# The row shares of an attention pair are turned as 128 rows and spread by four DMAs, and the plan gives out the attention's PSUM banks

## The chip, the cores and the metric

The kernel runs on one core of a Trainium2 chip. The metric is the device time of one execution in microseconds (us); the profile tells the span from the first to the last instruction, which is a little shorter. The engines are TensorE (PE; its weight loads stand as PEld), VectorE (DVE), ScalarE (ACT), GpSimd (POOL) and SyncE (SP), which here only issues DMAs.

## The reference

Causal attention over 2 batches, 12 heads, 448 tokens and head size 64, then two gated layers on the 896 tokens of 768 features. All data are float32.

```python
scores = q @ k.T / 8, masked above the diagonal
attn = exp(scores - max); attn = attn / (sum(attn) + 1e-9)
x = (attn @ v) with the heads side by side             # 896 x 768
x = (silu(x @ w_gate) * (x @ w_val)) @ w_out           # 768 -> 1536 -> 768
h = x @ w_in;  out = (h * clip(h + 3, 0, 6) / 6) @ w_out2   # 768 -> 2048 -> 768
```

## The kernel before

The kernel keeps float32 accuracy by cutting each operand into a rounded part and a rest (`hi`, `lo`) and summing three products. It has two stages: `attention()` and `mlps()`. The change is in the first.

Attention works on 12 pairs: two heads of one batch. A pair p goes through steps in a software pipeline over t:

- *Turn* (t = p - 2): q and k of the pair come in by DMA (`nat`), DVE turns them in 32 x 32 blocks (`f`), POOL or ACT rounds them (`qh`, `kh`) and POOL takes the rests (`ql`, `kl`). For the first two pairs PE does the turning.
- *Scores* (`sc`, t = p): 24 matmuls into PSUM banks, in three groups of rows. DVE adds the mask and takes the row maxima (`e<-sc,mask`), ACT takes the exponentials (`e<-e,m`) and the row sums (`s`).
- *Turned exponentials* (`tp`, t = p + 1): 20 PE transposes of 112 x 112, copied out of PSUM by ACT or DVE (`et`).
- *Product with v* (`pv`, t = p + 2): 16 matmuls into one bank. It is not yet divided by the row sums.
- *Shares* (`shares`, in `pv_parts`, between the second and the third product): POOL adds the epsilon to the 112 x 8 sums (`r`), DVE takes the reciprocal, POOL spreads each of the 8 columns over 64 columns (`rb`, 112 x 512), PE turns that in four transposes (`tr<-keep,rb`), and ACT copies the bank to SBUF (`rs`, 128 x 448). So rs holds, for each of the 128 rows (two heads of 64 features), the shares of the 448 tokens.
- *Last*: DVE multiplies the pv bank by rs (`xa<-pv,rs`, `xb<-pv,rs`) and frees the bank; rounding and rest give `x`, the first layer's operand.

From t = 7 on, four weight units of the first layer are also made ready (`first_unit`: one DMA `raw`, ACT, two shifts and joins on DVE, rounding, rest), and 36 of that layer's matmuls (`mm`) are woven into the last steps, as `ahead_parts`.

The order of the work is made before the kernel runs. `Plan.op` writes down each operation with its cost on the engines that may do it, what it reads and writes; `Plan.run` is a list scheduler that places them in time, on each engine the one that is due first, with a price for a change of kind on PE (`NEXT`, `WEIGHT`) and idle PE time in the first 21 us filled with matmuls of zeros. Every engine then runs its own list strictly in that order, so an instruction that waits holds up what stands behind it. SP's list of DMAs is also in that order. Before, an operation's PSUM bank is fixed when it is written down, from the list `idle` in program order.

Of the kernel before, what the change touches and what calls it, by code (L numbers as in the profile page):

```python
# [21 lines left out]
EB = 4  # L22
# [28 lines left out]
SLIP, WEIGHT = 0.1, 60.0  # L51
# [3 lines left out]
SOON = 6.0  # L55
CASTS = ("pool", "act")
HOLD, HEAD, LEND = 0.1, 3.0, 0.0
# [6 lines left out]
SHARED = ("vec", "pool")  # L64

# [16 lines left out]
class Spot:  # L82

    def __init__(self, make=None, place=None, real=None, ready=0.0):
        self.make, self.place, self.real, self.ready, self.after = make, place, real, ready, set()

# [6 lines left out]
class Plan:  # L93

    def __init__(self, in_order=("pe", "sp"), start=START, hold=0.0, ahead=0.0, alone=None, lend=None):
        self.ops, self.uses, self.on_place = [], {}, {}
        self.soon, self.kinds, self.by, self.alone = [], [], [], alone
# [3 lines left out]
    def op(self, where, call, reads=(), writes=(), port=False, wire=0.0, soon=None, kind=None, by=None):  # L101

        i, before, ready = len(self.ops), set(), 0.0
        for writing, spots in ((False, reads), (True, writes)):
            for s in spots:
                spot, part = s if isinstance(s, tuple) else (s, None)
                if spot not in self.uses:
                    self.uses[spot] = []
                    old = self.on_place.get(spot.place)
                    if old is not None:  # L110
                        spot.after = {j for _, j, _ in self.uses[old]}
                    if spot.place is not None:
                        self.on_place[spot.place] = spot
                before |= spot.after
                ready = max(ready, spot.ready)
                one = spot.place is not None and spot.place[0] is self.alone
# [5 lines left out]
        self.ops.append((where, call, before, ready, port, wire + LANDING if wire else 0.0))  # L122
        self.soon.append(soon)
        self.kinds.append(kind)
        self.by.append(by)

    def run(self, emit):
# [3 lines left out]
        for i, (_, _, before, _, _, _) in enumerate(ops):  # L131
            for j in before:
                after[j].append(i)
# [3 lines left out]
        for i, (where, _, _, _, _, _) in enumerate(ops):  # L137
            if "pe" in where:
                due[i] = clock
                clock += where["pe"]  # L140
        for i in reversed(range(n)):
# [6 lines left out]
            if self.by[i] is not None:  # L148
                due[i] = min(due[i], clock - self.by[i])
        left = [len(ops[i][2]) for i in range(n)]  # L150
        at = [
            ops[i][3] if self.soon[i] is None else max(ops[i][3], due[i] - self.soon[i]) for i in range(n)
        ]
        free_at, port_free, wire_free = dict(self.start), 0.0, 0.0
# [3 lines left out]
        while waiting:  # L158
            best = None
            for e in free_at:  # L160
# [14 lines left out]
                starts = {i: max(free_at[e], at[i], port_free if shared and ops[i][4] else 0.0) for i in mine}  # L175
                t = min(starts.values())
# [18 lines left out]
            if e == "pe":  # L195
                last = self.kinds[i]
                if self.fill is not None and t < self.fill[2]:
                    for x in range(int((t - free_at[e]) / self.fill[0] - 0.5)):
                        placed.append((free_at[e] + x * self.fill[0], len(placed), n, e))
                        filled += 1  # L200
# [5 lines left out]
            placed.append((t, len(placed), i, e))  # L206
            lag = LAG[e]
            if ops[i][5]:
                wire_free = max(wire_free, t + cost) + ops[i][5] - LANDING
                lag = wire_free + LANDING - t - cost  # L210
# [6 lines left out]
        for t, _, i, e in sorted(placed):  # L217
            emit(t, e, ops[i][1] if i < n else self.fill[1])
        self.placed = sorted(placed)
# [3 lines left out]
def tile_attention_glu_mlp(  # L223
# [118 lines left out]
    def attention():  # L342
        with ExitStack() as st:
# [4 lines left out]
            nc.vector.memset(zeros, 0.0)  # L348
            make_identity(nc, ident)
# [11 lines left out]
            plan = Plan(in_order=(), start=AT_START, hold=HOLD, ahead=HEAD, alone=banks, lend=LEND)  # L361
# [9 lines left out]
            def bank(use):  # L371
                n = idle.pop(0)
                return Spot(lambda: banks.tile([128, 512], F32, tag=f"bank{n}", name=use), (banks, n)), n
# [3 lines left out]
            def zero(e):  # L377
                e.matmul(idler()[:, :128], zeros, zeros, start=True, stop=True)

            plan.fill = ZERO, zero, UNTIL  # L380
# [11 lines left out]
            natq, natk, set_of, v_of, e_of, et_of, s_of = {}, {}, {}, {}, {}, {}, {}  # L392
            PAIR = 2 * S * D

            def load(p, src):
# [3 lines left out]
                for row, rows, head, half_ in ((32, 64, 0, 0), (0, 32, 0, 1), (96, 32, 1, 1)):  # L399
# [9 lines left out]
                        writes=[(t, row)], wire=0.6 if rows == 64 else 0.53, soon=SOON,  # L409
# [54 lines left out]
            def split(p, src, f):  # L464
# [4 lines left out]
                    lambda e: move(e, hi(), f()), reads=[f], writes=[hi], port=True,  # L469
# [4 lines left out]
                    reads=[f, hi], writes=[lo], port=True,  # L474
# [134 lines left out]
            def tp_parts(p):  # L609
# [29 lines left out]
                return [lambda j=j, ks=ks: turns(j, ks) for ks in ((0,), (1,), (2, 3)) for j in range(2)]  # L639

            def pv_parts(p):
# [4 lines left out]
                vt, ets, sm = v_of[p], et_of.pop(p), s_of.pop(p)  # L646
# [16 lines left out]
                def shares():  # L663
                    r, rb = take("r", 2, [C, 2, NC]), take("rb", 1, [C, NC, 2, D])
                    tr, bn = bank("tr")
                    rs = box["rs"] = take("rs", 1, [128, S])
                    op(
                        {"pool": 0.22},
                        lambda e: e.tensor_scalar(out=r(), in0=sm(), scalar1=EPS, scalar2=None, op0=ALU.add),
                        reads=[sm], writes=[r],  # L670
                    )
                    op({"vec": 0.19}, lambda e: e.reciprocal(out=r(), in_=r()), writes=[r])
                    op(
                        {"pool": 0.72},
                        lambda e: e.tensor_copy(
                            rb(), r().rearrange("p j c -> p c j").unsqueeze(3).to_broadcast([C, NC, 2, D])
                        ),
                        reads=[r], writes=[rb], port=True,
                    )

                    def work(eng):
                        for c in range(NC):
                            eng.transpose(
                                tr()[:, c * C : (c + 1) * C], rb()[:, c].rearrange("p j d -> p (j d)"), ident[:C, :C]
                            )

                    op({"pe": 0.4}, work, reads=[rb], writes=[tr], kind="tp")
                    op({"act": 0.44}, lambda e: e.copy(rs(), tr()[:, :S]), reads=[tr], writes=[rs])
                    idle.append(bn)

                def last():
                    o, rs = box["o"], box["rs"]
# [19 lines left out]
                        reads=[(t, b), (x, 0)], writes=[(x, 1)], by=BY_END if p == NPAIR - 1 else None, port=True,  # L712
# [8 lines left out]
                return [lambda kc=kc: product(kc) for kc in range(2)] + [shares] + [  # L721
# [5 lines left out]
            def first_unit(src, a, b, ready, by):  # L727
# [8 lines left out]
                op(  # L736
                    {"sp": 1.0},
                    lambda e: e.dma_start(out=raw().rearrange("p a b two -> p a (b two)"), in_=src),
                    writes=[raw], wire=4.0,
                )  # L740
# [5 lines left out]
                    reads=[raw], writes=[w],  # L746
                )
                for g in range(2):
                    h = slice(g * a // 2, (g + 1) * a // 2)
                    op(  # L750
                        {"vec": 0.3},
                        lambda e, h=h: e.tensor_scalar(
                            out=w()[:, h].bitcast(U32), in0=w()[:, h].bitcast(U32), scalar1=3, scalar2=None,
                            op0=ALU.logical_shift_left,
                        ),
                        writes=[(w, g)], port=True,
                    )
                    op(
                        {"vec": 0.55},
                        lambda e, h=h: e.scalar_tensor_tensor(  # L760
                            out=w()[:, h].bitcast(U32), in0=raw()[:, h, :, 0], scalar=29, in1=w()[:, h].bitcast(U32),
                            op0=ALU.logical_shift_right, op1=ALU.bitwise_or,
                        ),
                        reads=[raw], writes=[(w, g)], port=True,
# [21 lines left out]
            def ahead_parts():  # L786

                def step(u, kk):
                    wh, wl = made[u]
                    if kk == 0:  # L790
                        early.append(bank("mm"))
                    t, _ = early[u]
# [51 lines left out]
            plan.run(lambda t, engine, call: call(by[engine]))  # L844

    def mlps():
# [5 lines left out]
        nc.vector.memset(half, 0.5)  # L852
        nc.vector.memset(floor, -0.484375)
# [185 lines left out]
        def plain(f, ws):  # L1039

            g1[f] = take([128, NT], F32, f"g{f}")
            for b in range(B):
                got = []
                if f == 0 and b == 0:
                    got = [(here((t(), (banks, f"bank{n}"))), n) for t, n in early]
# [609 lines left out]
```

## Time and profile before

| | us |
|---|---|
| median of 3 runs (541.24 to 541.77) | 541.48 |
| the profiled execution | 541.52 |
| its span | 539.7 |

The profiled execution lies within the spread of the runs, and 1.8 us of it lie outside the span. In the profile an engine's busy time counts instructions from start to end; PE's ends are modelled, so its time is better read from the starts of its phases and from the chain. "x20" counts instructions merged in one row, "a<-b" is the tile written and the tiles read, and "<-" behind an idle time names what ended it.

### The profile page before, as it was taken

The page shows a single profiled execution, that of the slowest core. Times are in us where ns is not written, and L with a number is a line of the kernel's source. Part 1 is how long each engine was busy: PE and PEld are TensorE (multiplying, and loading weights), DVE is VectorE, ACT ScalarE, POOL GpSimd, SP SyncE. Part 2 cuts the span into 40 slices and gives each one's busy share as a digit, 9 for nine tenths or more (in the row PEclk, how much of TensorE's full clock was granted, in tenths as well). Part 3 has the DMA queues.
Part 4 walks back from the last instruction along what each step waited for, and adds up shares of the span by engine and source line. Part 5 has one row for each costly group of instructions (what it writes and reads, how often), then busy time and mean ns, then how long its engine had stood idle before and what let it go on. Part 6 is the DMA issues. An engine that isn't in the chain of part 4 may idle for free.

```text
span 539.7 us, 9039 instructions
## 1 busy us (share of the span) xinstructions
PE 534.0 (99%) x3146; PEld 490.4 (91%) x3146; DVE 457.6 (85%) x932; ACT 417.6 (77%) x876; POOL 146.1 (27%) x163
## 2 busy tenths in 40 slices
PE   8999999999999999999999999999999999999997
PEld 6777778999999999999999999999999999999997
DVE  4999998999788778779998889989888957599982
ACT  5999996887787778589967788899898756696560
POOL 1799987304000000030030243222231300000311
PEclk9999999999999999999999999999999999999999
DMA  9998504355545433332002354365353155510112
GB/s 220 254 226 222 132 25 142 106 166 191 182 133 188 140 133 123 115 118 78 2 0 80 123 177 128 119 191 161 118 162 131 41 181 188 176 60 1 60 44 103
DMA packets 58990, 69.34 MB, mean 128 GB/s; under 512 B 16960, under 2 KB 52544, under 8 KB 58944
## 3 DMA queue, kind: packets, MB, share of 16 engines
q1 hardware_dynamic: 58016, 68.53, 42.7%
q8 instruction: 25, 0.41, 0.3%
q10 hardware_dynamic: 928, 0.23, 0.2%
q14 instruction: 21, 0.17, 0.1%
HBM read 65.99 MB, written 2.75 MB: 127 GB/s over the span
## 4 chain that ended last, share of the span: by engine, by line
PE 97%; DVE 1%; DMA 1%; issue 0%; SPq 0%; DVEq 0%
PE mm L76 83%; PE pv L76 5%; PE tp L76 4%; PE sc L76 4%; PE tr L76 1%; DMA nat<-in_k_dram 1%; DVE out L76 0%; DVE e L76 0%; SPq L76 0%; DVE ql L76 0%; DVE kl L76 0%; PE zero L76 0%; DVE m L76 0%; DVEq L76 0%
## 5 line engine op out<-in xcount | busy, mean ns | idle before, releaser
L76 PE MATMUL mm<-x,a 128*128 128x448 f32 x396 | 85.9, 363 | 0.0
L76 PE MATMUL mm<-x,s 128*128 128x448 f32 x378 | 80.6, 363 | 0.0
L76 PEld LDWEIGHTS mm<-x,a 128*128 128x128 f32 x396 | 74.6, 189 | 5.3
L76 PEld LDWEIGHTS mm<-x,s 128*128 128x128 f32 x378 | 71.2, 188 | 5.1
L76 ACT ACTIVATE raw<-raw,half 128x768 uint32<-128x768 uint8 (+1 forms) x66 | 64.5, 980 | 0.0
L76 PE MATMUL mm<-t,s 128*128 128x448 f32 x270 | 57.8, 363 | 0.0
L76 PE MATMUL mm<-op 128*128 128x384 f32 x315 | 56.5, 336 | 0.0
L76 PEld LDWEIGHTS mm<-op 128*128 128x128 f32 x315 | 55.1, 188 | 0.0
L76 PEld LDWEIGHTS mm<-t,s 128*128 128x128 f32 x270 | 50.7, 188 | 3.8 <-DVE tmp L76 0.2
L76 PE MATMUL mm<-go,wo 128*128 128x448 f32 x252 | 51.2, 363 | 0.0
L76 PEld LDWEIGHTS mm<-go,wo 128*128 128x128 f32 x252 | 47.4, 188 | 3.5 <-issue 0.2
L76 ACT ACTIVATE e<-e,m 112x448 f32<-112x448 f32 (+3 forms) x96 | 49.7, 537 | 0.6 <-DVE m L76 0.6
L76 DVE CUSTOM_DVE_ANT_0 e<-sc,mask 112x336 f32<-112x336 f32 (+3 forms) x96 | 36.7, 447 | 1.9 <-PE sc L76 1.6
L76 DVE SCALAR_TENSOR_TENSOR v<-v,raw 128x768 uint32<-128x768 uint32 x36 | 34.4, 955 | 3.6 <-ACT raw L76 3.3
L76 ACT ACTIVATE w<-raw 128x768 f32<-128x768 f32 (+1 forms) x34 | 29.5, 868 | 8.7 <-DMA raw<-in_moe_w_out_dram 5.1
L76 ACT ACTIVATE v<-raw 128x768 f32<-128x768 f32 x36 | 32.5, 908 | 4.7 <-DMA raw<-in_moe_w_out_dram 2.6
L76 DVE SCALAR_TENSOR_TENSOR w<-w,raw 128x768 uint32<-128x768 uint32 (+1 forms) x30 | 27.2, 907 | 3.9 <-ACT raw L76 3.9
L76 PE MATMUL mm<-x,ws 128*128 128x448 f32 x144 | 30.1, 366 | 0.0
L76 PEld LDWEIGHTS mm<-x,ws 128*128 128x128 f32 x144 | 26.8, 189 | 2.2
L76 ACT COPY tmp<-mm 128x448 f32<-128x448 f32 x40 | 21.2, 531 | 9.1 <-PE mm L76 8.8
L76 ACT CAST op<-h 128x384 fp32r<-128x384 f32 x30 | 15.3, 511 | 15.3 <-PE mm L76 14.6
L76 DVE TENSOR_TENSOR tmp<-mm,tmp 128x448 f32<-128x448 f32 x30 | 18.5, 621 | 9.5 <-PE mm L76 8.5
(253 smaller groups left out, 1265.0 us busy)
## 6 DMA issues: line engine op xcount, KB each, us to landing
raw<-in_moe_w_out_dram SPq DMA_DIRECT2D x24, 768.0 KB, 4.3
raw<-in_moe_w_in_dram SPq DMA_DIRECT2D x16, 768.0 KB, 4.5
raw<-in_moe_w_gate_dram SPq DMA_DIRECT2D x12, 768.0 KB, 4.3
raw<-in_moe_w_val_dram SPq DMA_DIRECT2D x12, 768.0 KB, 4.3
raw<-in_moe_w_out_dram SPq DMA_DIRECT2D x6, 512.0 KB, 3.4
v<-in_v_dram SPq DMA_DIRECT2D x12, 224.0 KB, 5.3
out_dram<-out SPq DMA_DIRECT2D x14, 192.0 KB, 1.9
nat<-in_k_dram SPq DMA_DIRECT2D x10, 216.0 KB, 5.0
```

Source lines behind the costliest of these rows:

```text
L76: ins = call(*args, **kw)
```

## The change

1. The step `shares` moves from `pv_parts` to `tp_parts`, behind the six turnings: one step earlier in the pipeline.
2. For 11 of the 12 pairs POOL now spreads the 8 columns over 128 columns alone (`rr`; each column 16 times), one PE transpose turns them, ACT or DVE copies 128 x 112 numbers out (`row`), and four DMAs on SP, one for each of the four blocks of 112 tokens, read 32 of the 128 rows, each four times, into the 128 partitions of `rs`. The last pair keeps the four transposes and the copy on ACT.
3. `Plan.run` gives out the attention's 8 banks at planning time, with at most 6 held for scores and 5 for products; before, the order was fixed in advance.
4. The scheduler's constants change (`WEIGHT`, `SOON`, `HOLD`, `HEAD`), and kinds of work get a lead or a lag on their due times (`LEAD`). A DMA of shares is planned to land 5 us after its wire time.
5. In `first_unit` the DMA is cut in three, an ACT instruction takes the place of the two shifts on DVE. Two small memsets move ahead.

```diff
-SLIP, WEIGHT = 0.1, 60.0
+SLIP, WEIGHT = 0.1, 30.0
-SOON = 6.0
+SOON = 0.0
-HOLD, HEAD, LEND = 0.1, 3.0, 0.0
+HOLD, HEAD, LEND = 0.3, 5.0, 0.0
+LEAD = {
+    "load": -2.0, "hi": 1.0, "lo": -4.3, "sums": 1.0, "row": -3.0, "xlo": 2.0, "float": 4.0, "byte": 2.0, "join": 2.3,
+}
+MOST = {"sc": 6, "pv": 5}
+BY_BANK = 1
...
+        def opens(i, t):
+            k, kind = len(first[i]), self.kinds[i]
+            if len(open_) < k or held.get(kind, 0) + k > MOST.get(kind, self.n_alone):
+                return None
+            return max(t, sorted(open_)[k - 1][0])
...
+                def by_rows(r, tr, bn, rs):
+                    row, rr = take("row", 2, [128, C]), take("rr", 2, [C, 128])
+                    op(
+                        {"pool": 0.3},
+                        lambda e: e.tensor_copy(
+                            rr().rearrange("p (j k c) -> p j k c", j=2, c=NC),
+                            r().unsqueeze(2).to_broadcast([C, 2, 128 // NC // 2, NC]),
+                        ),
+                        reads=[r], writes=[rr], port=True,
+                    )
+                    op({"pe": 0.12}, lambda e: e.transpose(tr()[:, :C], rr(), ident[:C, :C]), reads=[rr], writes=[tr], kind="tp", lead=LEAD["row"])
+                    op({"act": 0.2, "vec": 0.22}, lambda e: move(e, row(), tr()[:, :C]), reads=[tr], writes=[row])
...
+                    def spread(e, c):
+                        src = row()[c : c + 1]
+                        e.dma_start(
+                            out=rs()[:, c * C : (c + 1) * C],
+                            in_=bass.AP(tensor=src.tensor, offset=src.offset, ap=[[NC * C, 128 // NC], [0, NC], [1, C]]),
+                        )
+
+                    for c in range(NC):
+                        op({"sp": 0.42}, lambda e, c=c: spread(e, c), reads=[row], writes=[(rs, c)], wire=0.25, land=5.0)
...
+                    if p < NPAIR - BY_BANK:
+                        by_rows(r, tr, bn, rs)
+                        return
...
-                return [lambda kc=kc: product(kc) for kc in range(2)] + [shares] + [
+                return [lambda kc=kc: product(kc) for kc in range(2)] + [
...
-                op(
-                    {"sp": 1.0},
-                    lambda e: e.dma_start(out=raw().rearrange("p a b two -> p a (b two)"), in_=src),
-                    writes=[raw], wire=4.0,
-                )
+                for g in range(3):
+                    h = slice(g * a // 3, (g + 1) * a // 3)
+                    op(
+                        {"sp": 0.45},
+                        lambda e, h=h: e.dma_start(out=raw()[:, h].rearrange("p a b two -> p a (b two)"), in_=src[:, h]),
+                        writes=[(raw, g)], wire=4.0 / 3,
+                    )
...
-                        {"vec": 0.3},
-                        lambda e, h=h: e.tensor_scalar(
-                            out=w()[:, h].bitcast(U32), in0=w()[:, h].bitcast(U32), scalar1=3, scalar2=None,
-                            op0=ALU.logical_shift_left,
-                        ),
```

## Rows read from the trace of the kernel before

**Rows 1.** The page: its first line, and the chain's shares by engine.
```profile
span 539.7 us, 9039 instructions
...
PE 97%; DVE 1%; DMA 1%; issue 0%; SPq 0%; DVEq 0%
```

**Rows 2.** The chain that ended last, 0 to 120 us: start, length, what.
```profile
27.08 0.53 PE tr L76 x4
27.61 1.92 PE tp L76 x20
29.53 1.88 PE sc L76 x24
31.41 2.04 PE pv L76 x16
33.45 0.54 PE tr L76 x4
...
84.28 0.38 PE tr L76 x4
...
91.46 28.68 PE mm L76 x141
```

**Rows 3.** Windows: stretch, length, busy of PE, PEld, DVE, ACT, POOL, clock, DMA.
```profile
33.98:40.36 6.38, 6.38 (x67) 4.90 (x65) 6.30 (x23) 6.38 (x24) 5.98 (x10) 1.00 0.93 213
...
84.66:91.46 6.80, 6.80 (x54) 5.33 (x51) 6.36 (x13) 3.66 (x8) 4.75 (x5) 1.00 0.36 116
...
104.20:110.60 6.40, 6.40 (x33) 5.96 (x33) 6.40 (x13) 4.12 (x8) 0.00 (x0) 1.00 0.67 209
```

**Rows 4.** Timeline: ACT's last read of pairs 3 and 8, PE's turning of them.
```profile
33.10 0.23 ACT L76 ACTIVATION_READ_ACCUMULATOR e<-e,m 112x1 f32 x1
...
33.82 2.08 PE L76 MATMUL tp<-keep,e 112*112 112x112 f32 x20
...
63.17 0.19 ACT L76 ACTIVATION_READ_ACCUMULATOR e<-e,m 112x1 f32 x1
...
65.69 2.08 PE L76 MATMUL tp<-keep,e 112*112 112x112 f32 x20
```

**Rows 5.** Groups by form, 0 to 130 us: busy, mean ns, idle before.
```profile
L76 ACT COPY et<-tp 112x336 f32<-112x336 f32 x30 | 11.7, 457 | 0.7 <-PE tp L76 0.5
...
L76 POOL COPY rb<-r 112x512 f32<-112x512 f32 x12 | 8.2, 686 | 0.8 <-PE tr L76 0.5 <-DVE r L76 0.2
...
L76 ACT ACTIVATE raw<-raw,half 128x768 uint32<-128x768 uint8 x7 | 7.0, 1001 | 0.0
...
L76 ACT COPY rs<-tr 128x448 f32<-128x448 f32 x12 | 6.4, 533 | 1.9 <-PE tr L76 1.8
...
L76 DVE TENSOR_SCALAR w<-w 128x384 uint32<-128x384 uint32 x8 | 2.8, 391 | 0.0
```

**Rows 6.** DMA, 0 to 95 us: a queue's packets, MB, share; issues: count, KB, us to landing.
```profile
q10 hardware_dynamic: 928, 0.23, 1.2%
...
v<-in_v_dram SPq DMA_DIRECT2D x12, 224.0 KB, 5.3
...
nat<-in_q_dram SPq DMA_DIRECT2D x20, 108.0 KB, 4.6
```

**Rows 7.** SP's timeline, 36 to 48 us.
```profile
45.18 0.88 SPq L76 DMA_DIRECT2D nat<-in_q_dram  x2
```

**Rows 8.** PE's timeline, 8 to 19 us: the matmuls of zeros.
```profile
9.77 1.29 PE L76 MATMUL zero<-zeros 128*128 128x128 bf16 x20
...
11.68 0.33 PE L76 MATMUL zero<-zeros 128*128 128x128 bf16 x3
...
15.27 0.50 PE L76 MATMUL zero<-zeros 128*128 128x128 bf16 x6
```

**Rows 9.** Timeline at the head of the next stage: DVE's last `t`, PE's first use.
```profile
116.96 1.16 DVE L76 TENSOR_TENSOR t<-xb,t 128x448 fp32r<-128x448 f32 x2 [0.33 <-ACT t L76]
...
118.77 3.79 PE L76 MATMUL mm<-t,s 128*128 128x448 f32 x18
```

More of the change, by code (lines that the diff above doesn't have):

```diff
@@ L93, with __init__, op @@
 class Plan:
-    def __init__(self, in_order=("pe", "sp"), start=START, hold=0.0, ahead=0.0, alone=None, lend=None):
+    def __init__(self, in_order=("pe", "sp"), start=START, hold=0.0, ahead=0.0, alone=None, lend=None, n_alone=0):
         self.ops, self.uses, self.on_place = [], {}, {}
-        self.soon, self.kinds, self.by, self.alone = [], [], [], alone
+        self.soon, self.kinds, self.by, self.lead, self.wish = [], [], [], [], []
+        self.alone, self.n_alone = alone, n_alone
         self.in_order, self.start, self.hold, self.ahead, self.lend = in_order, start, hold, ahead, lend
         self.fill = None
-    def op(self, where, call, reads=(), writes=(), port=False, wire=0.0, soon=None, kind=None, by=None):
-        i, before, ready = len(self.ops), set(), 0.0
+    def op(self, where, call, reads=(), writes=(), port=False, wire=0.0, soon=None, kind=None, by=None, lead=0.0, land=LANDING):
+        i, before, wish, ready = len(self.ops), set(), set(), 0.0
         for writing, spots in ((False, reads), (True, writes)):
@@ L113, in op @@
                         self.on_place[spot.place] = spot
-                before |= spot.after
+                one = spot.place is not None and spot.place[0] is self.alone
+                if one:
+                    wish |= spot.after
+                else:
+                    before |= spot.after
                 ready = max(ready, spot.ready)
-                one = spot.place is not None and spot.place[0] is self.alone
                 for p, j, w in self.uses[spot]:
@@ L121, in op @@
         before.discard(i)
-        self.ops.append((where, call, before, ready, port, wire + LANDING if wire else 0.0))
+        self.ops.append((where, call, before, ready, port, wire + land if wire else 0.0, wire))
         self.soon.append(soon)
@@ L125, in op @@
         self.by.append(by)
+        self.lead.append(lead)
+        self.wish.append(wish - before)
     def run(self, emit):
@@ L136, in run @@
         due = [None] * n
-        for i, (where, _, _, _, _, _) in enumerate(ops):
+        for i, (where, *_) in enumerate(ops):
             if "pe" in where:
@@ L149, in run @@
                 due[i] = min(due[i], clock - self.by[i])
+        for i in range(n):
+            for j in self.wish[i]:
+                after[j].remove(i)
         left = [len(ops[i][2]) for i in range(n)]
@@ L153, in run @@
         ]
+        due = [t - lead for t, lead in zip(due, self.lead)]
+        first, uses_of, users, over, held = [[] for _ in range(n)], [[] for _ in range(n)], {}, {}, {}
+        for s, uses in self.uses.items():
+            if self.n_alone and s.place is not None and s.place[0] is self.alone:
+                mine = sorted({j for _, j, _ in uses})
+                first[mine[0]].append(s)
+                users[s], over[s] = len(mine), 0.0
+                for j in mine:
+                    uses_of[j].append(s)
+        open_ = [(0.0, b) for b in range(self.n_alone)]
+        def opens(i, t):
[3 more added lines that the diff above has]
+            return max(t, sorted(open_)[k - 1][0])
         free_at, port_free, wire_free = dict(self.start), 0.0, 0.0
@@ L175, in run @@
                 starts = {i: max(free_at[e], at[i], port_free if shared and ops[i][4] else 0.0) for i in mine}
+                starts = {i: t for i, t in ((i, opens(i, t) if first[i] else t) for i, t in starts.items()) if t is not None}
+                mine = list(starts)
+                if not mine:
+                    continue
                 t = min(starts.values())
@@ L196, in run @@
                 last = self.kinds[i]
[L197 to L200, printed above, removed]
+                open_.sort()
+                k = len(first[i])
+                if self.fill is not None and t < self.fill[2] and len(open_) > k:
+                    at_, b = open_[k]
+                    at_ = max(at_, free_at[e])
+                    more = int((t - at_) / self.fill[0] - 0.5)
+                    if more > 0:
+                        call = self.fill[1](b)
+                        for x in range(more):
+                            placed.append((at_ + x * self.fill[0], len(placed), call, e))
+                        open_[k] = t + LAG[e], b
+                        filled += more
+                for s in first[i]:
+                    s.n = open_.pop(0)[1]
+                    held[self.kinds[i]] = held.get(self.kinds[i], 0) + 1
             free_at[e] = t + cost
@@ L206, in run @@
             placed.append((t, len(placed), i, e))
+            for s in uses_of[i]:
+                users[s] -= 1
+                over[s] = max(over[s], t + cost + LAG[e])
+                if not users[s] and not s.kept:
+                    open_.append((over[s], s.n))
+                    kind = self.kinds[min(j for _, j, _ in self.uses[s])]
+                    held[kind] -= 1
             lag = LAG[e]
             if ops[i][5]:
-                wire_free = max(wire_free, t + cost) + ops[i][5] - LANDING
-                lag = wire_free + LANDING - t - cost
+                wire_free = max(wire_free, t + cost) + ops[i][6]
+                lag = wire_free + ops[i][5] - ops[i][6] - t - cost
             for j in after[i]:
@@ L359, in attention @@
                 vset.append(t)
-            plan = Plan(in_order=(), start=AT_START, hold=HOLD, ahead=HEAD, alone=banks, lend=LEND)
+            plan = Plan(in_order=(), start=AT_START, hold=HOLD, ahead=HEAD, alone=banks, lend=LEND, n_alone=8)
             op = plan.op
@@ L408, in load @@
                         ),
-                        writes=[(t, row)], wire=0.6 if rows == 64 else 0.53, soon=SOON,
+                        writes=[(t, row)], wire=0.6 if rows == 64 else 0.53, soon=SOON, lead=LEAD["load"],
                     )
@@ new lines, in shares, with work @@
+                def shares():
+                    tr, bn = bank("tr")
+                    rs = rs_of[p] = take("rs", 2, [128, S])
+                    r = take("r", 2, [C, 2, NC])
+                    op(
+                        {"pool": 0.22},
+                        lambda e: e.tensor_scalar(out=r(), in0=sm(), scalar1=EPS, scalar2=None, op0=ALU.add),
+                        reads=[sm], writes=[r],
+                    )
+                    op({"vec": 0.19}, lambda e: e.reciprocal(out=r(), in_=r()), writes=[r], lead=LEAD["sums"])
+                    if p < NPAIR - BY_BANK:
+                        by_rows(r, tr, bn, rs)
+                        return
+                    wide = take("e", EB, [C, EW])
+                    rb = lambda: wide()[:, : 2 * NC * D].rearrange("p (c j d) -> p c j d", c=NC, j=2)
+                    op(
+                        {"pool": 0.72},
+                        lambda e: e.tensor_copy(
+                            rb(), r().rearrange("p j c -> p c j").unsqueeze(3).to_broadcast([C, NC, 2, D])
+                        ),
+                        reads=[r], writes=[wide], port=True,
+                    )
+                    def work(eng):
+                        for c in range(NC):
+                            eng.transpose(
+                                tr()[:, c * C : (c + 1) * C], rb()[:, c].rearrange("p j d -> p (j d)"), ident[:C, :C]
+                            )
+                    op({"pe": 0.4}, work, reads=[wide], writes=[tr], kind="tp")
+                    op({"act": 0.44}, lambda e: e.copy(rs(), tr()[:, :S]), reads=[tr], writes=[rs])
+                    idle.append(bn)
@@ L641, in pv_parts @@
+                sm = s_of.pop(p)
+                return [lambda j=j, ks=ks: turns(j, ks) for ks in ((0,), (1,), (2, 3)) for j in range(2)] + [shares]
             def pv_parts(p):
@@ L661, in product @@
                     op({"pe": w * 0.0018}, work, reads=[(et, kc) for et in ets] + [vt], writes=[o], kind="pv")
[L663 to L666, printed above, removed]
-                    op(
-                        {"pool": 0.22},
-                        lambda e: e.tensor_scalar(out=r(), in0=sm(), scalar1=EPS, scalar2=None, op0=ALU.add),
-                        reads=[sm], writes=[r],
-                    )
[L672 to L676, printed above, removed]
-                        ),
[L678 to L689, printed above, removed]
                 def last():
-                    o, rs = box["o"], box["rs"]
+                    o, rs = box["o"], rs_of.pop(p)
                     t = sum_of[id((sums if hp < HD else more_sums)[hp % HD][0])]
@@ L844, in attention @@
             plan.run(lambda t, engine, call: call(by[engine]))
+            idle[:] = plan.left
     def mlps():
@@ L1044, in plain @@
                 if f == 0 and b == 0:
-                    got = [(here((t(), (banks, f"bank{n}"))), n) for t, n in early]
+                    got = [(here((t(), (banks, f"bank{t.n}"))), t.n) for t, _ in early]
                 for wh, wl in ws[len(got) :]:
```

68 lines of the change are left out of this document (41 added, 27 removed).

## The prediction

> **What bounds the kernel now.** I read the page's chain first: 97% of the span runs along PE [rows 1]. The whole kernel is therefore a line of PE work, and a change is worth what it takes out of that line or puts into it as a wait. Next comes the chain in order of time, for the stretch in which the change lies. In the steady part of the attention PE goes through tr, tp, sc and pv without a gap: 0.53, 1.92, 1.88 and 2.04 us, and the next tr begins 6.37 us after the one before [rows 2]. Nothing but PE stands between two pairs. The attention hands over at 91.46 us, from where the chain is matmuls of the next stage alone [rows 2].
>
> The windows warn against stopping there. In one such pair, of 6.38 us, DVE is busy 6.30, ACT 6.38 and POOL 5.98 [rows 3]. If these were the bound too, shorter PE work would only turn into waiting. The timeline decides it: ACT finishes with pair 3 at 33.33 us and PE begins to turn that pair at 33.82; for pair 8 it is 63.36 and 65.69 [rows 4]. The lead grows from 0.5 to 2.3 us, so ACT takes (63.36 - 33.33) / 5 = 6.01 us a pair while PE takes 6.37. They are full because the plan hands them work early, not because PE waits for them. But their spare is only 0.36 us a pair, and that figure carries the argument below.
>
> **The change part by part.**
>
> *PE.* Three of four transposes go, in 11 pairs. In the tail, where no drained product is counted with them, four take 0.38 us [rows 2], 0.095 each; the 20 of tp give 1.92 / 20 = 0.096. In the steady part the group has 0.53, 0.15 more for the change of kind behind pv; this stays, since the one that is left still has to follow something. So 11 x 3 x 0.096 = 3.2 us leave the chain. Were the change of kind saved too, it would be 11 x (0.53 - 0.10) = 4.7; if the single transpose stands away from tp, its own two changes of kind cost 2 x 0.15 and eat the gain. I take 3.2: a transpose put beside tp is what a price on changes of kind asks for.
> The Trainium skill (TensorE: Matmul & The Clock Gate, LDWEIGHTS) has a weight load last its columns / 1.2 ns; with 128 columns that is an estimated 107 ns a transpose, by which the saving would be 3.5 us and the time 538.0. The trace does not agree, as the rate of four in 0.38 us is below that, and the sum goes by the trace.
>
> *ACT and DVE.* The copy `rs` of 533 ns [rows 5] leaves ACT 11 times, 5.9 us. In its place stands a copy of 112 columns, not in the trace: above nothing, below the 457 ns of 336 columns [rows 5]; I take 0.3, since a third of the columns is not a third of the time, hence 3.3 us on whichever engine is free. The period of ACT and DVE falls by about (0.53 - 0.3) / 2 = 0.1 us, from 6.01 to 5.9, still below PE's new 6.37 - 0.29 = 6.08. It hides, with 0.2 us a pair to spare; without that cover each 0.1 us over costs 1.1 us.
>
> *POOL.* Spreading 512 elements takes 686 ns [rows 5]; 128 take less, so up to 0.5 us a pair is freed there. POOL is not on the chain: nothing gained, nothing lost.
>
> *SP and the transfers.* There are 44 new DMAs on SP. Two issues of its own take 0.88 us [rows 7], so a pair adds 4 x 0.44 = 1.8 us to its 7 loads of 0.44, altogether 4.8 of 6.08: SP has room. The first of the four waits on SP for the row copy, and behind it the loads of later pairs stand too; they move back by that wait and 1.8 us, and their landing of 4.6 us [rows 6] is well within the three pairs that they run ahead. The pieces are 448 bytes, 512 of them a pair, a size not in the trace. On the second queue 928 packets, nearly all of 256 bytes, took 1.2% of 16 engines' 95 us, 20 ns each [rows 6]. A piece of 448 bytes then lies between 20 ns and, by bytes, 34 ns: 32 on each engine, 0.6 to 1.1 us a pair. In 34 to 40 us the DMA engines are busy to 0.93 [rows 3], and this much more makes landings later there, not PE slower.
>
> *The shares' way.* They now go through sum, reciprocal, spread, transpose, copy, issue and landing. The last DMA is issued 1.8 us behind the copy and lands 4.6 to 5.3 us later by the rows of loads of 108 and 224 KB [rows 6]; so the shares come about 7 us behind the copy, where before they were there with it. They start earlier by a step, one pair being 6.4 us. The product on DVE thus comes at most 2 or 3 us later, and holds its pv bank for so long. No PE instruction needs that product soon, so this is covered, with one exception below.
>
> *The plan's banks and constants.* PE waits for no bank in the steady part, where its chain has no gap [rows 2], so giving out banks otherwise has nothing to win there. At the start it may: PE runs 1.29 + 0.33 + 0.50 = 2.1 us of zeros between 9.77 and 15.77 us [rows 8], time that waits for DVE and ACT. Another order can recover at most that, or lose as much again. I take 0.
>
> *The weight units.* Two shifts of 391 ns go from DVE in each of four units, 8 x 0.391 = 3.1 us, and ACT gets four instructions of 1.0 us [rows 5]. ACT stands idle for 3.1 of the 6.80 us from 84.66 [rows 3], and covers most of it. The shifts matter for the head of the next stage: there DVE's last `t` ends at 118.12, and PE uses it at 118.77 [rows 9]. If PE comes 3.2 us sooner and DVE does not, 3.2 - 0.65 = 2.5 us are given back. DVE loses 3.1 us of work just ahead of this place, less what it takes of the row copies, and POOL, which may take such subtractions, does nothing at all in 104 to 110 us [rows 3]. So I count nothing lost.
>
> Sum: 541.5 - 3.2 = 538.3. The profiled execution took 541.52, its span of 539.7 and 1.8 us around it, and the median of the runs is 541.48, so no correction is needed.
>
> **The rivals.**
>
> *No change.* The transpose stands away from tp (2 x 0.15 a pair against 0.29 saved), or DVE keeps its date at the head of the next stage and 2.5 of 3.2 us are given back. For it: both covers are thin. Against it: the price on changes of kind, and DVE's relief. Time 541.0.
>
> *Slower.* The shares land behind the place that the plan gave the product. DVE works in order, so it stands still, and behind it the row maxima of the next scores, from which come the exponentials and PE's tp. DVE and ACT have 6.01 us of work; as soon as they lose more than 6.37 - 6.01 = 0.4 us a pair, the kernel is slower than before. With a loss of 1 us a pair the period is 7.01, and the time 541.5 + 11 x 0.64 = 548.5. For it: landings of 4.6 to 5.3 us on filled DMA engines, four in a row. Against it: the plan allows 5 us beside the wire time, so the typical landing is already in it.
> The Trainium skill speaks for this case (DMA: Bandwidth & Descriptors, Rules for kernel authors and Specifications): transfers under 64 KB are mostly overhead, and pieces under 512 bytes miss the line rate. The trace agrees in part: a load of 108 KB takes 4.6 us and one of twice the size 5.3, while 256-byte pieces cost no more than 20 ns. It bears on the delay, not on PE, and only where the product was planned too early.
>
> *More gain.* The 3.2 us come, and the order at the start gives back 1 to 2 of the 2.1 us of zeros, since banks are no longer bound to an order fixed in advance. Time 537.0. For it: these zeros are waits of PE. Against it: ACT and DVE are full from there on, and they, not banks, keep PE waiting.
>
> **How the numbers follow.** My forecast, 537.8 to 539.3 us, has 0.50; more gain 0.22; no change 0.15; slower 0.13. What a measurement can tell from no change is 0.2%, 1.1 us. Forecast and more gain lie beyond it, and a part of the no-change case (540.2 or so) too: faster 0.74, same 0.14, slower 0.12. The range takes in the bound of the zeros below (538.3 - 2.1 = 536.2) and the no-change case above, 541.3; it leaves out the slower case.
>
> **What would show it.** Right: in the chain a pair takes about 6.08 us, one transpose stands beside tp's twenty, and the stage is handed over near 88.3 us. Right on the delay: DVE's products show no idle time that a DMA of `rs` ended. Wrong: the period stays above 6.2; tp or sc waits for DVE; products wait for `rs`; or PE shows gaps at its first matmuls of the next stage, with DVE named as releaser. What the start gives or takes shows in the time of the tr that now stands at 27.08 [rows 2].

## The result, and the profile after

The changed kernel takes 548.94 us (545.66 to 549.69, six runs), the kernel before 541.45 (541.24 to 541.77) beside it: a ratio of 1.0125, with an interval of 1.0097 to 1.0153. It is slower, by 7.5 us. Times are medians throughout; a ratio is estimated over all runs of both kernels and need not be the quotient of the medians. The profiled execution took 549.11 us, its span 547.3, so 7.6 more than before.

The page of the changed kernel: its first line, the chain by engine, and the new DMAs' issues (count, KB, us to landing).

```profile
span 547.3 us, 9044 instructions
...
PE 82%; DVE 6%; DMA 5%; ACT 3%; SPq 2%; issue 1%; DVEq 0%; ACTq 0%
...
rs<-row SPq DMA_DIRECT2D x44, 56.0 KB, 2.6
```

PE had 97% of the chain [rows 1] and now has 82, and DMAs and SP's issues stand in it. That alone does not show a loss: an experiment below, one_issue, has PE at 86% and no loss. Where PE waits is shown by windows of 10 us, with the columns of [rows 3]:

```profile
30.00:40.00 10.00, 10.00 (x100) 7.06 (x100) 7.78 (x27) 9.90 (x36) 7.72 (x12) 1.00 0.64 172
40.00:50.00 10.00, 7.91 (x77) 5.52 (x73) 9.10 (x34) 7.25 (x25) 7.44 (x11) 1.00 0.72 203
...
70.00:80.00 10.00, 7.66 (x73) 5.49 (x71) 7.56 (x25) 8.20 (x24) 5.84 (x10) 1.00 0.91 243
80.00:90.00 10.00, 10.00 (x76) 7.23 (x75) 7.49 (x32) 8.30 (x27) 7.91 (x11) 0.83 0.69 169
```

PE stands still for 2.1 us in 40 to 50 and 2.3 in 70 to 80, and after the second of these stretches the granted clock is 0.83. The chain names what is late:

```profile
34.52 2.06 PE tp L81 x20
36.58 0.10 PE tr L81
...
37.81 3.75 DMA nat<-in_k_dram
41.55 0.58 DVE xa L81
...
58.62 2.41 DMA nat<-in_q_dram
...
70.22 5.43 DMA nat<-in_q_dram
75.67 2.10 DMA nat<-in_q_dram
...
78.90 0.55 DVE xa L81
79.50 1.42 PE tp L81 x9
80.92 3.33 PE pv L81 x16
```

The single transpose stands beside tp's twenty and takes 0.10, where four took 0.53 [rows 2]. But the chain now runs through loads of q and k. How a load comes to stop PE shows in the timelines of DVE and of PE:

```profile
40.74 0.94 DVE L81 STREAM_TRANSPOSE f<-nat 128x448 f32<-128x448 f32 x1 [1.49 <-DMA nat<-in_q_dram]
41.54 0.60 DVE L81 TENSOR_TENSOR xa<-pv,rs 128x448 f32<-128x448 f32 x1
```

```profile
42.28 1.80 PE L81 MATMUL tp<-keep,e 112*112 112x112 f32 x14 [1.69 <-DVE xa L81]
```

DVE waits in order for q of a later pair. Behind that in its list stands the product xa; the product frees a bank, and PE's tp waits for the bank. (The chain puts the same wait down to a load of k issued at 37.81; both views name a load.) The waits of 0 to 100 us (us in total, times, longest) show the sizes:

```profile
DVE f L81 <- DMA nat<-in_q_dram: 4.7, 6, 1.5
...
PE tp L81 <- DVE xa L81: 4.0, 2, 2.3
...
PEld tp L81 <- DVE xa L81: 2.6, 1, 2.6
...
DVE f L81 <- DMA rs<-row: 1.8, 1, 1.8
```

Only one of DVE's waits is put down to a landing of `rs`, and that instruction is f, which does not read rs; no product is shown waiting for its shares. Last, SP's timeline: it issues, back to back, what was to be on its way long before.

```profile
11.84 0.52 SPq L81 DMA_DIRECT2D nat<-in_k_dram  x1
17.52 2.57 SPq L81 DMA_DIRECT2D rs<-row  x4
...
48.30 2.54 SPq L81 DMA_DIRECT2D rs<-row  x4
50.88 1.05 SPq L81 DMA_DIRECT2D nat<-in_q_dram  x2
52.03 0.37 SPq L81 DMA_DIRECT2D v<-in_v_dram  x1
52.45 0.59 SPq L81 DMA_DIRECT2D nat<-in_k_dram  x1
53.08 0.59 SPq L81 DMA_DIRECT2D nat<-in_q_dram  x1
53.71 1.59 SPq L81 DMA_DIRECT2D nat<-in_k_dram  x2
55.41 2.53 SPq L81 DMA_DIRECT2D rs<-row  x4
```

From one pair's row DMAs to the next there are 7.1 us here, and SP is issuing in nearly all of them. The next table adds up the issues' durations in SP's timeline for every 10 us, with the time of the last issue of a load of q or k:

| SP issuing, us in | 10–20 | 20–30 | 30–40 | 40–50 | 50–60 | 60–70 | 70–80 | last load | time |
|---|---|---|---|---|---|---|---|---|---|
| before | 7.4 | 6.7 | 5.9 | 5.2 | 4.3 | 0.3 | 0.4 | 52.0 | 541.45 |
| changed | 4.4 | 8.5 | 9.2 | 8.7 | 9.1 | 9.1 | 8.3 | 75.7 | 548.94 |
| one_issue | 4.5 | 7.2 | 7.9 | 8.1 | 9.0 | 5.0 | 2.5 | 62.4 | 540.71 |
| idle_behind | 4.4 | 8.5 | 9.2 | 8.7 | 9.2 | 9.1 | 8.0 | 76.6 | 550.00 |
| extra_issues | 7.9 | 9.2 | 9.0 | 8.7 | 9.0 | 9.1 | 7.9 | 66.7 | 544.33 |
| from_2 | 7.8 | 2.3 | 9.2 | 8.6 | 8.8 | 8.7 | 8.9 | 71.0 | 546.06 |
| from_2_soon_6 | 6.9 | 8.7 | 9.1 | 8.2 | 9.0 | 9.2 | 7.2 | 64.5 | 542.15 |

Three pieces make up the 7.6 us of the span. PE's timelines show where the next stage begins, before and in the changed kernel, and a gap that is new:

```profile
91.39 1.89 PE L76 MATMUL mm<-x,ws 128*128 128x448 f32 x8
```

```profile
97.00 2.28 PE L81 MATMUL mm<-x,ws 128*128 128x448 f32 x10
...
128.50 1.67 PE L81 MATMUL mm<-t,s 128*128 128x448 f32 x7 [0.94 <-ACT mm L81]
```

The unbroken run of the next stage's matmuls begins at 97.0 rather than 91.4, 5.6 later. By then 12 rather than 18 of that stage's matmuls have been done early, and at 0.2 us from one to the next this is 6 x 0.2 = 1.2 more. The matmul ahead of 128.50 starts at 127.2, so 1.3 us lie between the two starts, 1.1 more than usual. That is 7.9, against 7.6 measured.

### The profile page after: what moved, and what is told of

Its sections match the earlier page's. It is cut to its first block, busy times and chain, and to the rows that moved or that the text cites. A ratio compares the mean times of both kernels' runs of the same rounds, so it can differ in the third digit from the quotient of the medians.

```text
span 547.3 us, 9044 instructions
## 1 busy us (share of the span) xinstructions
PE 534.9 (98%) x3108; PEld 486.8 (89%) x3108; DVE 456.3 (83%) x926; ACT 419.3 (77%) x878; POOL 141.5 (26%) x163
## 4 chain that ended last, share of the span: by engine, by line
PE 82%; DVE 6%; DMA 5%; ACT 3%; SPq 2%; issue 1%; DVEq 0%; ACTq 0%
PE mm L81 76%; DMA nat<-in_q_dram 3%; PE tp L81 2%; SPq L81 2%; PE sc L81 2%; PE pv L81 2%; ACT e L81 1%; DVE t L81 1%; DVE e L81 1%; DMA raw<-in_moe_w_gate_dram 1%; DVE w L81 1%; DMA nat<-in_k_dram 1%; DVE xa L81 1%; ACT w L81 0%; ACT raw L81 0%
## 5 line engine op out<-in xcount | busy, mean ns | idle before, releaser
L81 ACT ACTIVATE raw<-raw,half 128x768 uint32<-128x768 uint8 (+1 forms) x70 | 68.5, 982 | 0.0
L81 ACT ACTIVATE e<-e,m 112x336 f32<-112x336 f32 (+3 forms) x96 | 49.7, 531 | 4.3 <-DVE m L81 3.7
L81 DVE SCALAR_TENSOR_TENSOR w<-w,raw 128x768 uint32<-128x768 uint32 (+2 forms) x38 | 32.7, 867 | 4.1 <-ACT raw L81 4.0
L81 PE MATMUL tp<-keep,e 112*112 112x112 f32 x240 | 28.1, 265 | 5.5 <-DVE xa L81 4.0
L81 PEld LDWEIGHTS tp<-keep,e 112*112 112x112 f32 x240 | 23.3, 134 | 9.3 <-DVE xa L81 2.6
```

The costliest lines, as they stand in the source:

```text
L81: ins = call(*args, **kw)
```

## The experiments

**Which part of the change it is.** The first kernel keeps the plan's banks and the constants, the earlier shares and the weight units, but every pair has four transposes again; the other two keep the rows and alter what the plan is told.

```diff
# bank_all
-                    if p < NPAIR - BY_BANK:
+                    if 99 <= p < NPAIR - BY_BANK:
-                    wide = take("e", EB, [C, EW])
+                    wide = take("rb", 1, [C, 2 * NC * D])
# soon_6
-SOON = 0.0
+SOON = 6.0
# sp_cost
-                        {"sp": 0.5},            # a load
+                        {"sp": 0.6},
-    op({"sp": 0.42}, lambda e, c=c: spread(e, c), ...
+    op({"sp": 0.645}, lambda e, c=c: spread(e, c), ...
```

> All 12 pairs keep the four transposes and ACT's copy, so the rows and their 44 DMAs are gone; the earlier step of the shares, the banks from the plan and the constants stay. If SP's list is what costs (its DMAs take 6.4 us or more a pair against a period of 6.1, so loads come late), SP needs under 4 us a pair again and the time is 541 to 544 us. If the constants cost (loads asked for too late), it stays at 546 to 549. If the longer hold of the pv banks costs, 540 to 542.

> The loads may again be issued up to 6 us ahead of their due time; all else as after the change. If asking too late is the cause, the loads are early again and the time falls to 538 to 541 us. If SP's list is full, its sum is the same and only the first pairs gain: 545 to 548. If pv banks are the cause, no change: 548 to 549.

> The plan is told 0.645 us for a DMA of shares in place of 0.42 and 0.6 for a load of q or k in place of 0.5, as they measured; all else as after the change. If SP's list is the cause, a true cost lets the other engines be ordered around it: fewer waits for loads, but SP is still full, 543 to 547 us. If the constants or the banks are the cause, 547 to 550.

Measured: bank_all 543.21 us, ratio 1.0037 (1.0026 to 1.0049); soon_6 544.07, 1.0038 (1.0021 to 1.0055); sp_cost 548.64, 1.0127 (1.0106 to 1.0148). So without rows and DMAs the rest costs 1.8 us, and rows with their DMAs cost 5.7 where they were to gain 3.2. Allowing loads to be planned earlier gives 4.9 back; 544.07 lies between the figures of its expectation and decides for none. Telling the plan SP's true durations gives nothing. By its expectation that spoke for constants or banks, but bank_all keeps both and loses little, and so does the next kernel. That the plan found no room on a full list is my reading, not shown.

**Is it the number of issues?** In one_issue a pair's four DMAs become one with the same 512 pieces. It brings the shares of block 0 for all four blocks, so this kernel and the two after it leave out the shares of the other three; plan and order are those of the changed kernel. The other two put three DMAs of 64-byte pieces, which nobody reads, behind or ahead of it.

```diff
# one_issue
+                        if c:
+                            return
-  out=rs()[:, c * C : (c + 1) * C],
-  in_=bass.AP(..., ap=[[NC * C, 128 // NC], [0, NC], [1, C]]),
+  out=rs().rearrange("p (c t) -> p c t", c=NC),
+  in_=bass.AP(..., ap=[[NC * C, 128 // NC], [0, NC * NC], [1, C]]),
# idle_behind, in place of the return (idle_ahead: c != 3)
+                        if c != 0:
+  out=spare[:, c * 16 : (c + 1) * 16],
+  in_=bass.AP(..., ap=[[NC * C, 128 // NC], [0, NC], [1, 16]]),
```

> One DMA a pair fills the whole of rs, in the same 512 pieces of 448 bytes, from the rows of the first block alone (so the shares of the other three blocks of tokens are wrong); the plan is unchanged, and SP issues 11 DMAs where it issued 44. If SP's issuing is the cause, SP falls to about 4.5 us a pair and the time to 538 to 542 us. If the transfer itself, the late landing or the held banks are the cause, it stays at 546 to 549.

> The kernel of one_issue (one DMA of 512 pieces brings block 0's shares for all four blocks, so three of four blocks get wrong shares), with the same plan and order, and three DMAs of 64-byte pieces behind it, which bring part of the row to a tile that nobody reads. So SP issues 44 DMAs again, as in the changed kernel, while the shares arrive after the first of the four. Theory 1 (the time that SP's issues take, through the loads behind them): 547 to 549 us, loads late, tp waits for xa. Theory 2 (the shares' arrival after four landings, or the four transfers of 448-byte pieces side by side): 540 to 542.5, as one_issue (540.71).

> As idle_behind, but the three DMAs of 64-byte pieces stand ahead of the one that brings the shares (wrong ones likewise), so the shares arrive some 1.9 us later than there, about when the last of the four arrives in the changed kernel. Theory 1 (SP's time alone): the same as idle_behind within 1 us. Theory 2 (the products wait for the shares): 547 to 549 here, 5 or more above idle_behind.

Measured: one_issue 540.71 us, ratio 0.999 (0.9975 to 1.0005); idle_behind 550.0, 1.015 (1.012 to 1.0179); idle_ahead 551.07, 1.0175 (1.0137 to 1.0214). The 33 idle issues cost 9.3 us: all that one issue had gained (8.2), and a little more. Bytes and pieces of the shares are the same in one_issue and the changed kernel, so these are not the cause. Three issues more between the row and its shares change nothing that these runs can tell (550.0 against 551.07, with overlapping runs): the shares' delay is not the main cause either. The chain of one_issue shows the forecast's steady part:

```profile
33.34 2.06 PE tp L81 x20
35.40 0.10 PE tr L81
35.49 1.86 PE sc L81 x24
37.35 2.04 PE pv L81 x16
39.39 2.06 PE tp L81 x20
...
45.47 2.06 PE tp L81 x20
```

The period is 6.05 and 6.08 us. In idle_behind the loads are late at the same place as in the changed kernel; its chain has

```profile
37.26 3.99 DMA nat<-in_q_dram
...
42.17 0.61 DVE xa L81
```

**The same idle issues in other plans.** 44 idle DMAs of 64-byte pieces, four a pair as above, are added to bank_all and to the kernel before. They read a constant, so they wait for no row.

```diff
+                    for c in range(NC):
+                        op({"sp": 0.42}, lambda e, c=c: extra(e, c), reads=[rs], wire=0.25)
```

> As bank_all (all pairs by the bank, 543.2 us), with four more DMAs on SP for each of 11 pairs, in the same three-level form but with pieces of 64 bytes, from a constant into a tile that nobody reads. Nothing waits for their data, so only their issues cost. If SP's issues are the cause, 0.6 us each makes loads late here too: 546 to 550 us. If what cost was the wait for the shares' landing, the held banks or the transfer, it stays at 543 to 544.

> The kernel before with the same 44 idle DMAs on SP, and with its loads still issued up to 6 us ahead. If issues on SP cost in themselves, 543 to 546 us; if they cost only where loads are asked for late, 541.5 to 542.5.

Measured: extra_issues 544.33 us, ratio 1.0049 (1.0033 to 1.0064), only 1.1 over bank_all; before_extra 549.45 (543.85 to 551.0), 1.0127 (1.0083 to 1.0171). The first is near the figure that its expectation gave to other causes, and it speaks against SP's time as the whole cause: SP is as full there as in the changed kernel (the table), yet its last load goes out at 66.7 us rather than 75.7, since nothing stopped the list at 12 us. The comparison is not quite clean: its pairs keep four transposes, 0.29 us more of PE each, and so leave SP more time. before_extra is above both figures of its expectation. There the attention runs as before up to 65 us; then a weight's load is late, and ACT waits for it in order, until 72.84. Its waits of 60 to 100 us, and its window of 70 to 80:

```profile
ACT w L76 <- DMA raw<-in_moe_w_val_dram: 3.9, 1, 3.9
```

```profile
70.00:80.00 10.00, 7.70 (x51) 5.27 (x47) 5.66 (x24) 6.16 (x17) 5.54 (x6) 0.84 0.47 87
```

**SP's time, or the wait at the head of its list?** The first pair, or the first two, keep four transposes, so that no row DMA stands at 12 us; in the third kernel loads may also be planned earlier.

```diff
-                    if p < NPAIR - BY_BANK:
+                    if 1 <= p < NPAIR - BY_BANK:     # from_2: 2 <= p; pairs below spread by POOL, one block at a time
-SOON = 0.0
+SOON = 6.0                                           # from_2_soon_6 alone
```

> The changed kernel, but the first pair keeps four transposes (its shares spread by POOL in four pieces of 128 columns) and has no row DMAs; 40 of the 44 are left. In the changed kernel SP stood idle from 12.36 to 17.52 us behind the first pair's row, and filled 8.5 to 9.2 of every 10 us from 20 to 70. Theory A (that wait at the head of SP's list is what the full list never makes good): SP busy over 6 of 10 us in 10 to 20, loads some 5 us sooner, the last of q at 67 to 70 us, time 543 to 545.5. Theory B (the sum of the issues alone): four issues fewer are 2.6 us of SP, last load near 73, time 547 to 548.5.

> As from_1 with the first two pairs on four transposes; 36 row DMAs are left, and the first stands 28 us into the plan. Theory A: 542.5 to 545, hardly better than from_1. Theory B: four further issues fewer, 1 to 1.5 us less than from_1.

> from_2 with SOON at 6, so loads may be planned earlier, as before the change; the plan's end of the stage is 91.2 us, the earliest of these three. Both theories: the quickest version with right shares if the loads' lateness is all that was wrong, 539.5 to 542; if it stays over 543, something else than late loads costs time in it.

Measured: from_1 547.0 us, ratio 1.0109 (1.0092 to 1.0126); from_2 546.06, 1.0095 (1.0062 to 1.0128); from_2_soon_6 542.15, 1.0015 (0.9997 to 1.0032). Theory A failed as I had put it. Its signs on SP came in from_1 (7.9 us of 10 to 20, the last load at 70.1), but 547.0 is B's figure. The likely reason is in from_1's timeline of SP, where the wait is not gone but has moved to the next pair's row:

```profile
19.61 0.89 SPq L81 DMA_DIRECT2D nat<-in_q_dram  x2
25.58 2.56 SPq L81 DMA_DIRECT2D rs<-row  x4
```

Once SOON lets loads be planned ahead of that row, SP waits there for 2.1 us, where it waits for 7.3 in from_2; the last load goes out at 64.5, and the loss is gone but for 0.7 us, although 36 row DMAs are left, PE's period is the short one and SP is as full.

**Fewer issues.** two_blocks brings every block its own shares, by two transposes and two DMAs of 896-byte pieces a pair, with constants searched anew for the plan, SOON at 6 among them; one_issue_soon_6 is one_issue (block 0's shares for all) with SOON at 6; two_loads keeps the four row DMAs and brings q and k by two DMAs each rather than three.

```diff
# two_blocks
-  out=rs()[:, c * C : (c + 1) * C],
-  in_=bass.AP(..., ap=[[NC * C, 128 // NC], [0, NC], [1, C]]),
+  out=rs()[:, 2 * c * C : 2 * (c + 1) * C],
+  in_=bass.AP(..., ap=[[4 * C, 64], [0, 2], [1, 2 * C]]),
# two_loads
-  ap=[[NB * D, rows], [1, RUN]],
+  ap=[[32, 2], [NB * D, 32], [1, RUN]],
```

> Two transposes of 128 rows a pair, each row then holding two blocks of 112 tokens side by side, and two DMAs a pair with pieces of 896 bytes; the loads up to 6 us ahead, the plan told 0.62 us for a DMA of shares and 0.56 for a load, constants chosen anew for this order. Two transposes saved instead of three: 2.1 us on PE. If SP's list is the cause, SP has 4.7 us a pair and the time is 539 to 541.5 us. If the way of the shares over SBUF costs in itself, 544 to 548.

> One DMA a pair in place of four (wrong shares for three of the four blocks) and the loads up to 6 us ahead, both at once. If both cost through the same thing, SP's list being late, then with SP relieved the earlier loads add nothing: 539.5 to 541.5 us. If they were two causes, their gains of 8.2 and 4.9 us add up: 536 to 538.

> The changed kernel with all its row DMAs, but q and k of a pair come in by two DMAs each rather than three (one a head, 64 rows of 3,456 bytes, the same bytes; the features of a head in natural order), so that a pair has 5 loads rather than 7 on SP: 4 x 0.645 + 5 x 0.57 = 5.4 us of 6.08. Theory 1 (SP's time): much of the loss goes, 540 to 544 us, and few waits for q. Theory 2 (the rows' way itself): 547 to 549.

Measured: two_blocks 541.88 us, ratio 1.0004 (0.9995 to 1.0013); one_issue_soon_6 539.57, 0.9966 (0.9954 to 0.9979); two_loads 670.42, 1.2376 (1.2354 to 1.2398). Half the new issues, with constants to suit, bring the time back to that of before; what SOON alone gave of this, 4.9 in the changed kernel, is not told apart here. The gains of one issue (8.2) and of SOON (4.9) don't add: together they give 9.4, so they mend mostly the same thing. two_loads says nothing on the question, since it made the loads themselves slow; its window of 50 to 60 us:

```profile
50.00:60.00 10.00, 2.75 (x34) 1.81 (x30) 0.94 (x1) 2.05 (x10) 0.56 (x1) 0.81 0.13 51
```

No kernel that brings every block its own shares beat the one before.

## Why the prediction was wrong

**The step that failed** is "SP and the transfers", with its "4.8 of 6.08: SP has room". I took 0.44 us for every issue from two loads [rows 7], 1.8 for the four of the rows and 3.1 for the seven loads. In the stretch of SP's timeline above the four take 2.5 us, 0.60 each with 0.04 between two, and the seven 4.2: 0.37 to 0.59 each, and one of 1.1. With the gaps between them they fill 7.1 us a pair and not 4.8; without the long one it would be 6.6. PE's new period is 6.08. SP's timeline of the kernel before already has issues from 0.37 to 0.59 in 36 to 48 us, so two loads were too few to price them all. So loads fall behind pair by pair, and my "three pairs that they run ahead" are used up.

**And the wait on the row.** I named it and let the loads move back "by that wait and 1.8 us". It was 5.2 us at the first pair (12.36 to 17.52), and the full list does not make it good: the last load goes out at 75.7. That both take part in the loss is what the kernels show together: 33 issues fewer behind the same wait remove it (one_issue), and earlier loads on as full a list remove most of it (soon_6, from_2_soon_6), while a full list without a wait costs 1.1 us (extra_issues, with PE's longer pairs). How the 5.7 us divide between the two isn't settled. Nor is a full list alone always cheap: 44 idle issues cost 7.9 us in the kernel before, by a weight's load, and this is read from its waits, not tested by a kernel of its own.

The Trainium skill (DMA: Bandwidth & Descriptors, Issuing engines are not separate DMA queues) calls the time to initiate a DMA usually small beside the DMA itself. For one DMA the trace agrees only roughly, 0.60 us against 2.6 to landing; the eleven of a pair on one list are what filled it.

**PE: right.** One transpose of 0.10 beside tp, a period of 6.05 to 6.08 in one_issue, where 6.08 was forecast. Its attention is 2.3 us shorter than before: the unbroken run begins at 87.9 with 12 early matmuls done, so 91.4 - 87.9 - 6 x 0.2. That is 0.9 less than the 3.2 counted. In bank_all, with the new plan and four transposes, the run begins at 91.7 with 12 done, so against it one_issue gains 3.8.

**ACT, DVE, POOL: they do not bound PE, as said.** The copy of the row takes 0.25 to 0.26 us on either engine, 0.3 was taken; POOL's spreading takes 0.29, down from 0.69. The spare of 0.2 us a pair is not shown: in a pair of one_issue of 6.05 us ACT is busy for all 6.05 and DVE for 5.89, but PE has no gap there.

**The shares' way: covered, as said.** They land 2.6 us after issue, against 4.6 to 5.3 taken, and idle_ahead shows no price for delay that is clear of the spread of its runs. The 448-byte pieces, which the rival took for slow, landed sooner than any load of q, k or v in the changed kernel (3.4 to 4.4).

**Banks and constants: not nothing.** bank_all loses 1.8 us, near the 2.1 that the prediction allowed to be lost. It keeps the earlier shares and the new weight units too, so the 1.8 are not the banks' and constants' alone. Most of it lies in the attention, whose end is 0.3 later with 6 early matmuls fewer done, 1.5 us in all.

**The weight units: a part is given back**, which the prediction had held possible and counted as nothing. It had named DVE's last `t`; the chain of one_issue names a weight's load, which goes out only when DVE's `w` is done:

```profile
112.86 0.88 DVE w L81
...
113.80 4.25 DMA raw<-in_moe_w_gate_dram
...
118.08 0.90 ACT w L81
118.98 0.44 ACT mm L81
...
119.46 10.71 PE mm L81 x51
```

PE's matmul before that one starts at 118.08, so 1.4 us lie between two starts, and 1.2 of the 2.3 won are lost. In one_issue_soon_6 0.5 are lost at such a place (122.5). It comes to 539.6, so the forecast of 538.3 was 1.3 too low even where loads are early and SP's list is eased.

**The slower rival** had the time, 548.5, and the right last links, but the time by luck, from a loss of 1 us a pair that was set as an example: DVE stands still in order, and PE's tp comes late. Its cause was wrong. The rival had the shares' landing wait on filled DMA engines, and "products wait for `rs`" as its sign; what DVE waited for were loads of q and k. I gave it 0.13, because I had priced the shares' landing and not SP's list.

## What to carry to other kernels

A queue's issuing is an engine's work: add up every issue of a period with the duration of its own kind, and set the sum against the period that you hope for, not the present one. A DMA that waits for a computed tile must not stand ahead of loads on the same in-order list unless the list has the time to make the wait good. To price issues apart from bytes, put idle DMAs with tiny pieces in the same places of the same order.

## What the runs showed of the hardware

Issues of the row DMAs in the changed kernel and of the idle ones in idle_behind (ns, least/median/most):

```profile
L81 SPq DMA_DIRECT2D rs<-row x44: 523/602/1572, 17.5 to 91.4; - x44
```

```profile
L81 SPq DMA_DIRECT2D spare<-row x33: 524/602/632, 18.0 to 92.7; - x33
```

- The issue's time on SP hardly depended on the bytes of these copies: 0.602 us (median) for 128 pieces of 448 bytes and the same 0.602 for 128 of 64 bytes, 0.66 to 0.68 (medians of one_issue and idle_behind) for 512 of 448. An issue can also hold SP up: in two_loads, whose transfers were slow, a load of v at 25.84 kept SP for 4.01 us, against 0.37 above.
- two_loads had the outermost dimension of its source at 2, and the DMA engines were busy at 0.13 of 16, 51 GB/s, where the changed kernel has 0.66 to 0.72 in 40 to 60 us. The Trainium skill (DMA: Bandwidth & Descriptors, Why a DMA increments its semaphore by 16 and not by 1) has the slowest dimensions' common factor, up to 16, set the number of engines. That is 2 of 16 here, an estimated 0.125 where such DMAs alone run, and the trace agrees.
- A wait can cost twice. In the changed kernel PE was idle for 2.3 us of 70 to 79.5, and then the granted clock was 0.61 from 80.92 to 84.25, most of it at 1.2 rather than 2.4 GHz: sixteen matmuls of pv took 3.33 us rather than 2.04. After the 2.1 us of 40 to 50 it stayed at 1.00. The runs with a mean clock of 1.0 took 545.66 and 546.69, those with 0.993 to 0.997 took 548.77 to 549.69, so some 3 us of the 7.5 go with the clock; that the clock alone makes them is not shown.
